# All 36 weight-sum pieces made in blocks 1 and 2 of a fused attention and gated feed-forward kernel, none in the first pair

## The chip, the cores and the metric

The kernel runs on one core of one Trainium2 chip. The metric is the device time of one execution in microseconds (us), the median of several executions; lower is better. Engines are named as the profile names them: PE (TensorE matmul) and PEld (its weight loads), DVE (VectorE), ACT (ScalarE), POOL (GpSimd) and SP (SyncE, whose queue SPq issues every DMA of this kernel).

## The reference: what is computed

Chunked attention (chunks of 64 tokens, 8 batches, 8 heads, 576 tokens, head size 64), and its output, as 4608 tokens of 512 numbers, through a gated feed-forward layer with 1536 hidden features. All in float32:

```python
scores = scale * np.matmul(q_c, k_c.transpose(0, 1, 2, 4, 3))
scores = scores - np.max(scores, axis=-1, keepdims=True)
attn = np.exp(scores)
attn = attn / (np.sum(attn, axis=-1, keepdims=True) + 1e-09)
out = np.matmul(attn, v_c)
...
x = np.ascontiguousarray(attn_out.transpose(0, 2, 1, 3)).reshape(B * S, H * D)
gate = 1.0 / (1.0 + np.exp(-(x @ w_gate)))
val = x @ w_val
return (gate * val @ w_out).astype(np.float32)
```

## The kernel before

**Tiling.** The 4608 tokens are 9 blocks of 512. Float32 products are made from a high and a low part of each operand, three matmuls for one product. Blocks 0, 1 and 2 go through the feed-forward layer directly: for each of 12 feature groups f, `up` makes the gate in PSUM buffer g0 (12 matmuls) and the value in g1 (12 matmuls), one buffer each, and `down` (12 matmuls) adds the group to four output banks `acc`. Blocks 3 to 8 go as three pairs n = 0, 1, 2, in which two blocks of tokens, two halves of features and two halves of d_model are multiplied with seven products in the place of eight (L563 and L712). For that the weights are needed in sums and differences as well, kept in DRAM.

**The pieces.** `keep_sums` (L436) makes these weight sums in 36 pieces. A piece is two or three additions on DVE (L452, or L456 and L459), five instructions on POOL (L461, L462, L463, L465, L466) and two or four DMAs on SP's queue (L470 into `sums`, L474 into `stream`). Pieces 1 to 24 are for the gate and value weights, 25 to 36 for the output weights. Two pieces share a tile `a_val`, and there are two places for it, "spare" and "p1", one buffer each, used by turns: the first DVE addition of an odd piece waits until the two pieces that had that place before are through POOL and their DMAs have landed. `a_high` takes a buffer of the tag "ob" (two buffers), which the block outputs (`evacuate`, L399) use too.

**What sets the order.** PE, DVE and ACT issue in the order in which the program is written, in blocks 1 and 2 (`rest`, L909) and in the pairs (`pairs`, L934). POOL and SP are put in order by a scheduler in blocks 1 and 2, and stand as written in the pairs. In blocks 1 and 2 a step is one feature group and has two halves; after each half `tick` and `insert` hand out parts of the attention of later blocks (`flow`, L743), and then `keep` (L901) is called with the number of pieces that are wanted by then. With h the number of the half step, counted from 2 at block 1's first, the number wanted is

```python
keep(9 * (h - 2) // 10 if h < 21 else 16 if h < 24 else min(30, h - 7))
```

so that 16 pieces are made in block 1, none while its outputs leave (h from 21 to 23), and pieces 17 to 30 in block 2, up to h = 37. The last six are made in the first pair, one or none at each of its steps, with `late=True`: the high part then stands in the same tile, and the stores are put off to the next step (`put`, L485).

**What stands around it.** `hidden` (L370) is the chain of one step: gate in g0, sigmoid on ACT (L373, frees g0), value in g1, product on DVE (L376, frees g1), high part on ACT (L379), low part on DVE (L381). At the end of block 2 the first pair's operands are made from the attention output `raw`: `differ` (L525, DVE), `operands` (L541 DVE, L545 ACT) and `lower` (L553, DVE). All of these stand in DVE's and ACT's queues between the steps' own instructions.

Of the kernel before, what the change touches and what calls it, by code (L numbers as in the profile page):

```python
# [8 lines left out]
F32 = mybir.dt.float32  # L9
F32R = mybir.dt.float32r  # L10
# [5 lines left out]
P = 128  # L16
D = 64
NB = 9
TB = 512
# [46 lines left out]
PRODUCTS = (1, 6, 2, 7, 5, 4, 3)  # L66
# [3 lines left out]
def chunk_attn_moe(ctx: ExitStack, tc: tile.TileContext, q, k, v, w, out, outt):  # L70


    nc = tc.nc

    const = ctx.enter_context(tc.tile_pool(name="const", bufs=1))
    wp = ctx.enter_context(tc.tile_pool(name="wp", bufs=1))
    xp = ctx.enter_context(tc.tile_pool(name="xp", bufs=4))
    ap2 = ctx.enter_context(tc.tile_pool(name="ap2", bufs=2))
    mp = ctx.enter_context(tc.tile_pool(name="mp", bufs=2))
# [12 lines left out]
    kp = ctx.enter_context(tc.tile_pool(name="kp", bufs=1))  # L92
# [13 lines left out]
    wt, raws, whole, made, spare, arrivals = {}, {}, {}, {}, {}, []  # L106
# [314 lines left out]
    given, sums, vals = {}, {}, {}  # L421
    stream = dp.tile([P, 7, 6, 512], F32, name="stream")

    def keep_given(p, which):

        if which == 2:
            for r, f, i in ((1, 2 * p, 0), (2, 2 * p + 1, 0), (4, 2 * p + 1, 1)):
                nc.sync.dma_start(
                    stream[:, PRODUCTS.index(r), p].rearrange("p (a n) -> p a n", a=2),
                    wt[f, 2][:, :, i * 256:(i + 1) * 256].bitcast(F32))  # L430
            return
        t = given[p, which] = dp.tile([P, 3, 2, 256], F32, name=f"given{p}{which}")
        for n, (f, k) in enumerate(((2 * p, 0), (2 * p, 1), (2 * p + 1, 1))):
            nc.sync.dma_start(t[:, n], wt[f, which][:, :, k * 256:(k + 1) * 256].bitcast(F32))

    def keep_sums(p, which, c, late=False):  # L436

        if c == 0 and which < 2:
            sums[p, which] = dp.tile([P, 2, 2, 2, 256], F32, name=f"sums{p}{which}")
        if late or c == 0:  # L440
            pool, tag = ((wp, "spare"), (kp, "p1"))[(c if late else 2 * p + which if which < 2 else p) % 2]
            vals[0] = pool.tile([P, 2, 4, P], F32, tag=tag, name="a_val")
        if late:
            val, high = vals[0][:, 0], vals[0][:, 1].rearrange("p s n -> p (s n)").bitcast(F32R)
        else:
            val, high = vals[0][:, c], mp.tile([P, TB], F32R, tag="ob", name="a_high")
        for n in range(2):
            f = 2 * p + n
            if which < 2:
                parts = wt[f, which].rearrange("p a (k c n) -> p a k c n", k=2, c=2)[:, :, :, c].bitcast(F32)  # L450
                dst = val[:, 1:3] if n else val[:, 0::3]
                nc.vector.tensor_tensor(out=dst, in0=parts[:, 0], in1=parts[:, 1], op=ALU.add)  # L452
                continue
            parts = wt[f, 2].rearrange("p a (i c n) -> p a i c n", i=2, c=2)[:, :, :, c].bitcast(F32)
            if n == 0:
                nc.vector.tensor_tensor(out=val[:, 0:2], in0=parts[:, 0], in1=parts[:, 1], op=ALU.add)  # L456
            else:
                for i, at in enumerate((3, 2)):
                    nc.vector.tensor_tensor(out=val[:, at], in0=parts[:, 0, i], in1=parts[:, 1, i], op=ALU.add)  # L459
        flat = val.rearrange("p s n -> p (s n)")  # L460
        nc.gpsimd.tensor_tensor(out=val[:, 1], in0=val[:, 1], in1=val[:, 2], op=ALU.add)  # L461
        nc.gpsimd.tensor_tensor(out=val[:, 0], in0=val[:, 1], in1=val[:, 0], op=ALU.subtract)  # L462
        nc.gpsimd.tensor_tensor(  # L463
            out=val[:, 2:4], in0=val[:, 2:4], in1=val[:, 0:1].broadcast_to([P, 2, P]), op=ALU.subtract)
        nc.gpsimd.tensor_copy(high, flat)  # L465
        nc.gpsimd.tensor_tensor(out=flat, in0=flat, in1=high.bitcast(F32), op=ALU.subtract)  # L466
        def store():
            for a, t in enumerate((high.bitcast(F32), flat)):
                if which < 2:
                    nc.sync.dma_start(sums[p, which][:, :, c, a], t.rearrange("p (h n) -> p h n", h=2))  # L470
                    continue
                for i, r in enumerate((6, 7)):
                    at = PRODUCTS.index(r)
                    nc.sync.dma_start(  # L474
                        stream[:, at:at + 4:3, p, c * 256 + a * P:c * 256 + (a + 1) * P],
                        t[:, i * 256:(i + 1) * 256].rearrange("p (s n) -> p s n", s=2))

        if late:
            stores.append(store)
        else:  # L480
            store()

    stores = []

    def put():  # L485
        while stores:
            stores.pop(0)()

    places = ["u8", "u9", "u10", "u11", "u7"]

# [384 lines left out]
    def insert(upto=4 * NB, pieces=0):  # L875


        if now["item"] in ("S", "then") or (
                now["item"] in ("A", "AS") and now["unit"] < upto and now["ticks"] >= now["since"] + pieces):
            if now["item"] in ("A", "AS"):  # L880
                release()
            advance()
# [9 lines left out]
    def step(m, f, span):  # L892
        pending.append(hidden(m, f, spans[span]))

    def finish():
        down(*pending.pop(0))
# [1 line left out]
    kept = [(p, which, c) for p in range(6) for which in range(2) for c in range(2)]  # L898
    kept += [(p, 2, c) for p in range(6) for c in range(2)]

    def keep(wanted, late=False):  # L901
        while len(kept) > 36 - wanted:
            p, which, c = kept.pop(0)
            if c == 0 and which < 2:
                with tc.issue_after(arrivals[-1].ins):
                    keep_given(p, which)
            keep_sums(p, which, c, late)

    def rest():  # L909
        with tc.issue_after(arrivals[-1].ins):  # L910
            for p in range(6):
                keep_given(p, 2)
        for m in range(1, FIRST_PAIR):
            upto = 4 * (m + 2) if m == 1 else 4 * (m + 3)
            for f in range(2 if m == 1 else 0, NF):
                if m == 2 and f == 7:
                    now["early"] = now["open"] = now["late"] = 0
                step(m, f, "")
                x = 2 * (12 * m + f - 13)
                for part in range(2):  # L920
                    if part:
                        finish()
                    tick(SHARES[m])
                    insert(upto, 1)
                    h = x + part
                    keep(9 * (h - 2) // 10 if h < 21 else 16 if h < 24 else min(30, h - 7))
                if m == 2:
                    if f == 8:
                        for which in range(2):
                            load_group(0, 0, which)  # L930
        with tc.manual_schedule(engines={mybir.EngineType.Pool, mybir.EngineType.SP}):
            pairs(keep)

    def pairs(keep):  # L934
        for n in range(3):
            now["joined"], now["late"], now["up"] = True, n, n
            upto = 4 * (FIRST_PAIR + 2 * n + 4)
            order = [(p, which) for p in range(6) for which in range(2)]
            due(n, 5)
            for i, (p, which) in enumerate(order):  # L940
                if i + 1 < len(order) and i > 0:
                    load_group(n, *order[i + 1])
                put()
                if pending:
                    banks[n, "z"] = sole(n, p, which)
                    while pending:
                        finish()
                first(n, p, which)
                if i == 0:
                    due(n, 7)  # L950
                if i == 11:
                    now["early"] = n + 1
                if i:
                    tick(SHARES["first"], "first")
                    last(n, *order[i - 1])
                    if i == 10:
                        ending = outward(n, lambda: (last(n, *order[-1]), gate()))
                        next(ending)
                    late = 30 + (0, 1, 2, 3, 3, 4, 5, 6)[min(i, 7)]
                    if n == 0 and i % 2:  # L960
                        keep(late, True)
                    tick(SHARES["last"] if i < 11 else 1.2, "last")
                    gate()
                    if n == 0:
                        keep(late, True)
                middle(n, p, which, lambda: i and insert(upto, 1))
                if i == 10:
                    next(ending)
                if i == 11:
                    now["open"] = n + 1  # L970
                if 0 < i < 11:
                    tick(SHARES["middle"], "middle")
            next(ending, None)
# [39 lines left out]
```

## Time and profile before

| | |
|---|---|
| time, median of 3 runs | 885.11 us (883.43 to 886.03) |
| the profiled execution's own time | 887.66 us |
| its span | 885.8 us |
| PE busy | 875.8 us (99%) |
| DVE, ACT, POOL busy | 625.4, 401.4, 267.1 us |
| block 1, about | 146 to 250 us from the span's start |
| block 2, about | 250 to 346 us |
| the first pair, about | 346 to 529 us |
| pieces 1 to 30 on POOL | 162.6 to 326.2 us |
| pieces 31 to 36 on POOL | 360.8 to 431.3 us |

The profile is one execution; 1.9 us of its time lie outside the span. A PE that is busy is not PE at its peak, since matmuls are pipelined, so a lost microsecond shows in three places: as idle time ahead of a PE instruction, as a group of matmuls that takes longer than the same group elsewhere, and as a granted clock below 1.00. In rows of the timeline and of the groups, the bracket or last column tells how long the engine sat idle ahead of the instruction and what ended that.

### The profile page before, as it was taken

What the parts mean: (1) busy time and instruction counts of PE and PEld (TensorE: products, weight loads), DVE (VectorE), ACT (ScalarE), POOL (GpSimd) and SP (SyncE); (2) the same over time, 40 slices, a digit from 0 to 9 for tenths busy, and PEclk for the clock granted to TensorE, in tenths of its full rate; (3) what the DMA queues carried; (4) which work ended last, traced back from release to release, by engine and by line L of the source; (5) the groups of instructions that cost most, each with busy time, mean ns of one, the idle gap of its engine ahead of it and who ended that gap; (6) DMA issues with size and microseconds to landing.
All of it is one profiled execution on the core that took longest, in us unless ns stands there. A gap on an engine that the chain in (4) does not pass through costs nothing.

```text
span 885.8 us, 15559 instructions
## 1 busy us (share of the span) xinstructions
PE 875.8 (99%) x6050; PEld 718.7 (81%) x6050; DVE 625.4 (71%) x908; ACT 401.4 (45%) x706; POOL 267.1 (30%) x329
## 2 busy tenths in 40 slices
PE   8999999999999999999999999999999999999998
PEld 4888888888888888878888888888888888888886
DVE  6999963588668865757768957666589654335874
ACT  6897662345535443345554523555245221123341
POOL 0000000497948960676720002253400002432000
PEclk9999999999999999999999999999999999999999
DMA  8675389946355477677865567666345685654453
GB/s 316 233 249 202 116 282 343 303 135 196 128 167 167 132 206 270 204 274 231 291 226 191 214 217 257 238 240 237 134 178 216 210 307 173 209 202 139 182 216 140
DMA packets 84506, 189.77 MB, mean 214 GB/s; under 512 B 7248, under 2 KB 45648, under 8 KB 80592
## 3 DMA queue, kind: packets, MB, share of 16 engines
q1 hardware_dynamic: 84432, 188.77, 61.7%
q8 instruction: 48, 0.79, 0.4%
q14 instruction: 26, 0.21, 0.1%
HBM read 146.28 MB, written 42.47 MB: 213 GB/s over the span
## 4 chain that ended last, share of the span: by engine, by line
PE 93%; DMA 3%; DVE 2%; issue 0%; ACT 0%; SPq 0%; DVEq 0%
PE g L357 22%; PE d L712 19%; PE cy L563 16%; PE cz L563 11%; PE acc L392 11%; PE cx L563 10%; PE av L212 2%; DMA w_raw<-w_in 2%; PE sc L197 2%; DMA wr<-sums 1%; DMA wr<-given 1%; DVE xc L553 0%; PE tp L281 0%; DVE raw L525 0%; DVE pr L823 0%
## 5 line engine op out<-in xcount | busy, mean ns | idle before, releaser
L357 PE MATMUL g<-xt,w 128*128 128x512 f32 (+1 forms) x960 | 206.2, 370 | 0.8 <-DVE xt L301 0.6
L357 PEld LDWEIGHTS g<-xt,w 128*128 128x128 f32 x960 | 167.5, 188 | 32.3 <-DVE xt L301 0.9
L712 PE MATMUL d<-hd,wd 128*128 128x512 f32 x756 | 172.5, 389 | 0.1
L712 PEld LDWEIGHTS d<-hd,wd 128*128 128x128 f32 x756 | 141.8, 188 | 30.3 <-DVE hd L692 0.9
L563 PE MATMUL cy<-xc,wr 128*128 128x512 f32 x648 | 159.2, 389 | 0.2 <-DMA wr<-sums 0.2
L563 PEld LDWEIGHTS cy<-xc,wr 128*128 128x128 f32 x648 | 121.6, 188 | 25.8 <-DMA wr<-sums 0.6
L563 PE MATMUL cz<-xc,wr 128*128 128x512 f32 x432 | 111.1, 393 | 0.3 <-DVE u L620 0.2
L563 PE MATMUL cx<-xc,wr 128*128 128x512 f32 x432 | 111.2, 393 | 0.0
L392 PE MATMUL acc<-w,hx 128*128 128x512 f32 x432 | 105.3, 392 | 0.0
L563 PEld LDWEIGHTS cz<-xc,wr 128*128 128x128 f32 x432 | 81.8, 190 | 18.3 <-DVE u L620 0.6
L563 PEld LDWEIGHTS cx<-xc,wr 128*128 128x128 f32 x432 | 80.8, 188 | 17.1
L392 PEld LDWEIGHTS acc<-w,hx 128*128 128x128 f32 x432 | 80.1, 188 | 16.8
L461 POOL TENSOR_TENSOR a_val<-a_val 128x128 f32<-128x128 f32 x36 | 19.7, 547 | 214.1 <-DVE a_val L452 162.8
L838 POOL COPY pt<-pr 32x256 f32<-32x256 f32 x86 | 35.9, 418 | 156.8 <-DVE pr L827 153.1
L691 ACT CAST hd<-hid 128x1024 fp32r<-128x1024 f32 x48 | 49.9, 1051 | 49.2 <-PE d L712 33.2
L579 ACT COPY s1u<-cx 128x512 f32<-128x512 f32 x36 | 21.1, 586 | 106.3 <-PE cx L563 101.9
L692 DVE TENSOR_TENSOR hd<-hid,hd 128x1024 fp32r<-128x1024 f32 x48 | 58.4, 1221 | 12.4 <-ACT hd L691 12.2
L591 POOL TENSOR_TENSOR hid<-u,hid 128x512 f32<-128x512 f32 x15 | 19.5, 1301 | 142.4 <-DVE u L620 141.7
L581 DVE TENSOR_TENSOR s1u<-cy,s1u 128x512 f32<-128x512 f32 x36 | 24.7, 685 | 39.1 <-PE cy L563 39.1
L838 ACT COPY pt<-pr 32x256 f32<-32x256 f32 x110 | 44.3, 403 | 13.1 <-DVE pr L827 11.6
L641 ACT ACTIVATE hid<-hid 128x512 f32<-128x512 f32 x54 | 32.4, 628 | 34.9 <-DVE hid L635 28.9
L620 DVE TENSOR_TENSOR hid<-cz,u 128x512 f32<-128x512 f32 x18 | 12.4, 691 | 49.6 <-PE cz L563 49.5
(118 smaller groups left out, 1144.8 us busy)
## 6 DMA issues: line engine op xcount, KB each, us to landing
wr<-sums SPq DMA_DIRECT2D x72, 512.0 KB, 5.3
wd<-stream SPq DMA_DIRECT2D x30, 1024.0 KB, 4.6
w_raw<-w_in SPq DMA_DIRECT2D x36, 512.0 KB, 4.6
wr<-given SPq DMA_DIRECT2D x36, 512.0 KB, 4.3
qt<-q_in SPq DMA_DIRECT2D x18, 512.0 KB, 4.9
kt<-k_in SPq DMA_DIRECT2D x18, 512.0 KB, 5.8
vt<-v_in SPq DMA_DIRECT2D x18, 512.0 KB, 4.1
given<-w SPq DMA_DIRECT2D x36, 256.0 KB, 4.3
```

The source lines that it names most:

```text
L357: nc.tensor.matmul(ps[:, tok], lhsT=wt[f, which][:, wpart, c:c + P], rhs=x[:, part, i, tok], start=n == 0, stop=n == 11)
L392: nc.tensor.matmul(acc[m, t], lhsT=hx[:, ts], rhs=wt[f, 2][:, wpart], start=f == 0 and i == 0, stop=f == NF - 1 and i == 2,)
L461: nc.gpsimd.tensor_tensor(out=val[:, 1], in0=val[:, 1], in1=val[:, 2], op=ALU.add)
L563: nc.tensor.matmul(bank, lhsT=lhs(wpart, c), rhs=x[:, part, c], start=start and k == 0, stop=stop and k == 5, skip_group_check=True)
L579: nc.scalar.copy(s1, x)
L581: nc.vector.tensor_tensor(out=u2, in0=y, in1=s1, op=ALU.add)
L591: eng.tensor_tensor(out=h, in0=value, in1=h, op=ALU.mult)
L641: nc.scalar.activation(h, h, AF.Sigmoid)
L691: nc.scalar.copy(t[:, 0], at)
L692: nc.vector.tensor_tensor(out=t[:, 1], in0=at, in1=t[:, 0].bitcast(F32), op=ALU.subtract)
L712: nc.tensor.matmul(bank, lhsT=w[:, o:o + P], rhs=x[:, part], start=p == 0 and opening and i == 0, stop=p == 5 and i == 2, skip_group_check ...
L838: copy = (lambda eng, dst=pb[dst, :, c, i, :], src=ps[src, h::2, k, :]: eng(dst, src))
```

## The change

`keep` is called in blocks 1 and 2 with other numbers: h pieces after half step h up to 20, 20 while block 1's outputs leave, and from h = 24 on h - 3, until 36 are made at h = 39. The first half step makes two pieces, each further one makes one. The part that made pieces in the first pair is removed, with the late form of `keep_sums` and the stores that were put off. Nothing else of the program is changed; line numbers behind the edit are lower by up to 20 (L452 is L449, L456 is L453, L525 is L511).

```diff
-    def keep_sums(p, which, c, late=False):
+    def keep_sums(p, which, c):
...
-        if late or c == 0:
-            pool, tag = ((wp, "spare"), (kp, "p1"))[(c if late else 2 * p + which if which < 2 else p) % 2]
+        if c == 0:
+            pool, tag = ((wp, "spare"), (kp, "p1"))[(2 * p + which if which < 2 else p) % 2]
             vals[0] = pool.tile([P, 2, 4, P], F32, tag=tag, name="a_val")
-        if late:
-            val, high = vals[0][:, 0], vals[0][:, 1].rearrange("p s n -> p (s n)").bitcast(F32R)
-        else:
-            val, high = vals[0][:, c], mp.tile([P, TB], F32R, tag="ob", name="a_high")
+        val, high = vals[0][:, c], mp.tile([P, TB], F32R, tag="ob", name="a_high")
...
-        def store():
-            for a, t in enumerate((high.bitcast(F32), flat)):
...
-        if late:
-            stores.append(store)
-        else:
-            store()
+        for a, t in enumerate((high.bitcast(F32), flat)):
+            if which < 2:
+                nc.sync.dma_start(sums[p, which][:, :, c, a], t.rearrange("p (h n) -> p h n", h=2))
+                continue
...
-                    keep(9 * (h - 2) // 10 if h < 21 else 16 if h < 24 else min(30, h - 7))
+                    keep(h if h < 20 else 20 if h < 24 else min(36, h - 3))
...
-            pairs(keep)
+            pairs()
...
-                put()
...
-                    late = 30 + (0, 1, 2, 3, 3, 4, 5, 6)[min(i, 7)]
-                    if n == 0 and i % 2:
-                        keep(late, True)
                     tick(SHARES["last"] if i < 11 else 1.2, "last")
                     gate()
-                    if n == 0:
-                        keep(late, True)
```

How this moves the instructions is shown at three places.

DVE near the end of block 2, before: `hf` and `hx` are the products and low parts of the steps, `raw` and `xc` the first pair's operands. The first row is the product of feature group 8.

```order
L376 TENSOR_TENSOR hf<-g_3683,hf 128x512
L381 TENSOR_TENSOR hx<-hf,hx 128x512
L525 TENSOR_TENSOR raw<-raw 128x2x512
L376 TENSOR_TENSOR hf<-g_3740,hf 128x512
L381 TENSOR_TENSOR hx<-hf,hx 128x512
L525 TENSOR_TENSOR raw<-raw 128x2x512
L553 TENSOR_TENSOR xc<-raw,xc 128x1024 x3
L541 TENSOR_TENSOR raw<-raw 128x2x512
```

The same stretch of DVE in the changed kernel:

```order
L376 TENSOR_TENSOR hf<-g_3737,hf 128x512
L381 TENSOR_TENSOR hx<-hf,hx 128x512
L453 TENSOR_TENSOR a_val<-w 128x256
L456 TENSOR_TENSOR a_val<-w 128x128 x2
L511 TENSOR_TENSOR raw<-raw 128x2x512
L453 TENSOR_TENSOR a_val<-w 128x256
L456 TENSOR_TENSOR a_val<-w 128x128 x2
L376 TENSOR_TENSOR hf<-g_3821,hf 128x512
L381 TENSOR_TENSOR hx<-hf,hx 128x512
L511 TENSOR_TENSOR raw<-raw 128x2x512
L539 TENSOR_TENSOR xc<-raw,xc 128x1024 x3
L527 TENSOR_TENSOR raw<-raw 128x2x512
```

Two pieces, 35 and 36, now stand between the low part of group 8 and the product of group 9; ahead of the first row the two orders have the same kinds of rows back to the start of block 2, with pieces numbered four higher.

SP's queue at the end of block 2, before: the stores of pieces 29 and 30, a load of v, and the loads `wr` of the first pair's first weights.

```order
L474 DMA stream<-a_high 128x2x128 x2
L474 DMA stream<-a_val 128x2x128 x2
L178 DMA vt<-v_in 128x1024
L474 DMA stream<-a_high 128x2x128 x2
L474 DMA stream<-a_val 128x2x128 x2
L501 DMA wr<-given_1865 128x1024
L504 DMA wr<-sums_1869 128x1024
L501 DMA wr<-given_1865 128x512
L504 DMA wr<-sums_1869 128x1024
```

The same place in the changed kernel, from the stores of piece 33 on:

```order
L470 DMA stream<-a_high 128x2x128 x2
L470 DMA stream<-a_val 128x2x128 x2
L178 DMA vt<-v_in 128x1024
L470 DMA stream<-a_high 128x2x128 x2
L470 DMA stream<-a_val 128x2x128 x2
L487 DMA wr<-given_1820 128x1024
L490 DMA wr<-sums_1824 128x1024
L470 DMA stream<-a_high 128x2x128 x2
L470 DMA stream<-a_val 128x2x128 x2
L470 DMA stream<-a_high 128x2x128 x2
L470 DMA stream<-a_val 128x2x128 x2
L487 DMA wr<-given_1820 128x512
```

The stores of pieces 35 and 36 now stand between the first two `wr` loads and all later ones.

SP's queue in the first pair, before, at the step whose attention loads (`vt`, `qt`, `kt`) come second in the pair:

```order
L501 DMA wr<-given_2459 128x512
L504 DMA wr<-sums_2463 128x1024
L474 DMA stream<-a_val 128x2x128 x4
L178 DMA vt<-v_in 128x1024
L170 DMA qt<-q_in 128x1024
L172 DMA kt<-k_in 128x1024
```

The same step in the changed kernel:

```order
L487 DMA wr<-given_2265 128x512
L490 DMA wr<-sums_2269 128x1024
L178 DMA vt<-v_in 128x1024
L170 DMA qt<-q_in 128x1024
L172 DMA kt<-k_in 128x1024
```

The four stores of a late piece are gone from this step, as at five others. PE's and ACT's orders are the same row for row in both kernels.

## Rows read from the trace of the kernel before

**Rows 1.** The page's first part: busy time, share of the span, instructions

```profile
PE 875.8 (99%) x6050; PEld 718.7 (81%) x6050; DVE 625.4 (71%) x908; ACT 401.4 (45%) x706; POOL 267.1 (30%) x329
```

**Rows 2.** Chain that ended last, end of block 2: start us, us, what

```profile
325.11 2.23 DVE raw L525
327.34 3.48 DVE xc L553 x3
330.82 1.15 DVE raw L541
...
332.95 0.60 ACT hf L373
...
333.59 5.73 PE g L357 x24
```

**Rows 3.** Timeline of DVE, blocks 1 and 2: start us, us, what [idle before]

```profile
159.76 0.69 DVE L376 TENSOR_TENSOR hf<-g,hf 128x512 f32<-128x512 f32 x1 [3.40 <-PE g L357]
...
254.84 0.65 DVE L376 TENSOR_TENSOR hf<-g,hf 128x512 f32<-128x512 f32 x1
...
312.39 1.02 DVE L456 TENSOR_TENSOR a_val<-w 128x256 f32<-128x256 f32 x1 [2.45 <-DMA stream<-a_val]
...
314.00 0.68 DVE L456 TENSOR_TENSOR a_val<-w 128x256 f32<-128x256 f32 x1
...
315.55 0.68 DVE L376 TENSOR_TENSOR hf<-g,hf 128x512 f32<-128x512 f32 x1
...
317.95 1.47 DVE L525 TENSOR_TENSOR raw<-raw 128x1024 f32<-128x1024 f32 x1
322.66 0.69 DVE L376 TENSOR_TENSOR hf<-g,hf 128x512 f32<-128x512 f32 x1 [3.24 <-PE g L357]
```

**Rows 4.** Timeline of POOL, blocks 1 and 2

```profile
198.42 1.81 POOL L838 COPY pt<-pr 32x256 f32<-32x256 f32 x4
...
221.14 1.85 POOL L838 COPY pt<-pr 32x256 f32<-32x256 f32 x4 [3.08 <-DVE pr L827]
...
242.76 1.29 POOL L466 TENSOR_TENSOR a_val<-a_val,a_high 128x512 f32<-128x512 f32 x1
...
316.18 1.30 POOL L466 TENSOR_TENSOR a_val<-a_val,a_high 128x512 f32<-128x512 f32 x1
...
324.64 1.61 POOL L466 TENSOR_TENSOR a_val<-a_val,a_high 128x512 f32<-128x512 f32 x1
```

**Rows 5.** Timeline of SP's queue; then landings of L474's stores, 315 to 320 us

```profile
317.50 0.89 SPq L474 DMA_DIRECT2D stream<-a_val  x2
...
DMA to landing us min/median/max: 1.9/2.3/2.6
```

**Rows 6.** DVE groups by shape: L381, L525 at 162-326, L541 at 322-342, L684 anywhere

```profile
L381 DVE TENSOR_TENSOR hx<-hf,hx 128x512 fp32r<-128x512 f32 x18 | 17.6, 977 | 13.7 <-ACT hx L379 13.7
...
L525 DVE TENSOR_TENSOR raw<-raw 128x1024 f32<-128x1024 f32 x2 | 3.8, 1890 | 0.0
...
L541 DVE TENSOR_TENSOR raw<-raw 128x1024 f32<-128x1024 f32 x3 | 3.7, 1218 | 0.0
...
L684 DVE TENSOR_TENSOR hd<-hid,hd 128x512 fp32r<-128x512 f32 x30 | 19.6, 684 | 0.7 <-ACT hd L683 0.5
```

**Rows 7.** Timeline of PE in the first pair; its chain; windows with PEclk

```profile
385.30 1.65 PE L563 MATMUL cz<-xc,wr 128*128 128x512 f32 x6 [0.17 <-DVE u L620]
...
393.23 0.39 PE L197 MATMUL sc<-kt,qt 64*64 64x64 f32 x10 [1.65 <-issue]
...
393.62 2.07 PE cx L563 x6
395.69 2.48 PE cz L563 x6
398.17 1.36 PE cx L563 x6
...
395.00:396.00 1.00, 1.00 (x4) 0.74 (x3) 0.00 (x0) 0.27 (x1) 0.92 (x2) 0.50 0.67 262
```

**Rows 8.** Chain that ended last, where block 1's outputs leave

```profile
253.21 5.44 PE g L357 x24
```

More of the change, by code (lines that the diff above doesn't have):

```diff
@@ L466, in keep_sums @@
         nc.gpsimd.tensor_tensor(out=flat, in0=flat, in1=high.bitcast(F32), op=ALU.subtract)
-        def store():
-            for a, t in enumerate((high.bitcast(F32), flat)):
[L469 to L476, printed above, removed]
-        if late:
-            stores.append(store)
-        else:
-            store()
[L483 to L487, printed above, removed]
+        for a, t in enumerate((high.bitcast(F32), flat)):
+            if which < 2:
+                nc.sync.dma_start(sums[p, which][:, :, c, a], t.rearrange("p (h n) -> p h n", h=2))
+                continue
+            for i, r in enumerate((6, 7)):
+                at = PRODUCTS.index(r)
+                nc.sync.dma_start(
+                    stream[:, at:at + 4:3, p, c * 256 + a * P:c * 256 + (a + 1) * P],
+                    t[:, i * 256:(i + 1) * 256].rearrange("p (s n) -> p s n", s=2))
     places = ["u8", "u9", "u10", "u11", "u7"]
@@ L899, in chunk_attn_moe, with keep @@
     kept += [(p, 2, c) for p in range(6) for c in range(2)]
-    def keep(wanted, late=False):
+    def keep(wanted):
         while len(kept) > 36 - wanted:
@@ L906, in keep @@
                     keep_given(p, which)
-            keep_sums(p, which, c, late)
+            keep_sums(p, which, c)
     def rest():
@@ L931, in rest, with pairs @@
         with tc.manual_schedule(engines={mybir.EngineType.Pool, mybir.EngineType.SP}):
-            pairs(keep)
-    def pairs(keep):
+            pairs()
+    def pairs():
         for n in range(3):
```

## The prediction, made before the changed kernel was run

> **What bounds the kernel now.** First the page's busy times: PE is busy for 875.8 of 885.8 us [rows 1]. No microsecond of DVE, ACT or POOL counts unless PE comes to wait for it, so the question is not how much work is moved (none is removed) but where PE's cover is thin. Second the chain of work that ended last, which is PE nearly throughout. The place in blocks 1 and 2 where it leaves PE is 322.6 to 333.6 us, at the end of block 2 [rows 2]: DVE makes L525, three L553 and an L541 back to back, ACT then casts and does the sigmoid L373 of feature group 10, and only then may PE write g0 for group 11, at 333.59. The start of that chain is DVE's product of group 9 at 322.66, which waited 3.24 us for PE [rows 3]. So DVE has 3.24 us of slack just ahead of 322.66 and none behind it, up to 333.59. Third, PE in the first pair, where six pieces are made now: it waits 0.17 us for a DVE result at 385.30, and 1.65 us at 393.23 for nothing that the profile shows; behind that gap its granted clock is 0.50, the 1.2 GHz level, and two groups of six matmuls take 2.07 and 2.48 us where the next takes 1.36 [rows 7].
>
> **What the change removes.** Six late pieces leave the first pair: on DVE each costs about 1.6 us (piece 29 from 312.39 to 314.00, piece 30 from there to 315.55 [rows 3]), on POOL about 4.1 us: five pieces and five `pt` copies run from 221.14 to 242.76 + 1.29 = 244.05, 22.9 us [rows 4]; the copies, at 1.85 us for four, are 2.3 of it, and (22.9 - 2.3) / 5 = 4.1. That is 10 us of DVE and 25 us of POOL, beside a PE that waited for DVE there for 0.17 us [rows 7]. I credit 0.2. The 1.65 us gap and the 1.83 us behind it (2.07 + 2.48 - 2 x 1.36 [rows 7]) are named by the profile as no one's; PE's order, row for row, is unchanged, and the loads of v, q and k beside the gap stay. I take it to stay, credit 0, and keep -3.5 as the other end.
>
> **Early pieces.** Three pieces come in the first two steps of block 1, where DVE still waits 3.40 us for PE [rows 3]; their 4.8 us spread over two steps. Nothing on PE, since it does not wait for DVE there. Loads of q and k in SP's queue now stand behind stores of pieces 1 to 5, and are used a step or more later: 0.
>
> **Block 1.** Four pieces more are made by the pause. From the `pt` copies at 198.42 to those at 221.14 there are now five pieces and not four, and five took 22.9 us elsewhere [rows 4]: POOL is through at 198.42 + 22.9 = 221.3, where the copies now start at 221.14 after 3.08 us of idleness. POOL's slack is used up and it is 0.2 us late. Behind that, both orders have five pieces up to the pause, so piece 20 ends 0.2 us later than piece 16 does now. On it hangs a chain: store of the piece, the load of v behind it in SP's queue, four output stores, DVE's output copy, and then the product L376 at 254.84, ready at 255.49. PE wants it for the next value matmuls, 2.72 us into the 24 that start at 253.21 [rows 8], at 255.93. Cover 0.44 against 0.2 late: I take 0. The other end, should five pieces take 1 us more, is a wait of 0.8.
>
> **End of block 2.** From the start of block 2 to the low part of group 8, DVE's order has the same rows with pieces numbered four higher, so I read piece 28's times for 32. Then pieces 35 and 36 stand where DVE was idle, with L525 between them. Piece 35 needs the place "p1" from pieces 31 and 32. Piece 28's last POOL instruction runs from 316.18 to 317.48 [rows 4], its two last stores are issued from 317.50 to 318.39, and such stores land 1.9 to 2.6 us after issue, median 2.3 [rows 5]; the second, issued about 317.95, lands at 320.2. The same wait is seen on piece 29 now: 2.45 us, ended by such a store [rows 3]. So DVE stands idle from 317.95 to about 320.3, and then does piece 35 (1.6), L525 (1.47) and piece 36 (1.6): 325.0. The product of group 9 starts at 325.0 and not at 322.66: **2.3 us late**. Behind the waiting addition in DVE's queue stand exactly the instructions of the chain that ends at PE. Without the wait for the place the three would end at 317.95 + 4.7 = 322.65, just in time; it is the wait, not the work, that costs.
>
> To this comes POOL. Now it is done with piece 30 at 326.25 [rows 4]; with two more pieces it works to 326.25 + 2 x 4.1 = 334.5, all through the chain, which runs beside an idle POOL now. DVE instructions with two inputs in SBUF are slower beside a busy POOL: L381 takes 977 ns there and its twin L684 684 (+0.29), L525 1890 where L541 of the same shape takes 1218 (+0.67) [rows 6]. Three L553 and one L541 are newly exposed. Ends: 4 x 0.29 = 1.2 and 4 x 0.67 = 2.7; L525 is the nearest by shape but is two instances, L381 is eighteen, so I take the middle, **1.9**. Together g0 comes free 2.3 + 1.9 = 4.2 us later, and PE, which already waits at 333.59, has no cover. ACT's and DVE's other work shifts alike and adds nothing.
>
> The Trainium skill's page "SBUF — State Buffer", section "Who interferes with whom", gives the mechanism: a DVE instruction with two SBUF inputs contends with a GpSimd instruction that reads SBUF, and whoever holds the shared port keeps it for its whole instruction. The trace agrees that such instructions are longer and not by how much: by that rule each of the four could be held for a whole L466 of 1.3 us, 5.2 in all, and the time by it would be 3.3 us above mine.
>
> After a gap of 1.65 us PE's clock fell and cost 1.83 us [rows 7]. After one of 4.2 us I expect the same, **1.8**; the other end is 0, since matmuls of full size and not small ones precede this gap.
>
> The later `wr` loads stand behind the stores of pieces 35 and 36, at about 335 us; the first of them to be used, beyond the two ahead of those stores, is wanted about 350 by PE's order. No cost.
>
> **Sum.** 4.2 + 1.8 - 0.2 = +5.8 us. On the profiled execution: 887.66 + 5.8 = 893.5. That execution lies 2.55 us above the median of the runs; on the median, 885.11 + 5.8 = **890.9 us**. With the low ends (2.3 + 1.2 - 0.2) it is 888.4, with the high ones (2.3 + 2.7 + 1.8 - 0.2) 891.7.
>
> **The rivals.**
> - *The delay does not reach PE.* If the stores of piece 32 land by 318 us or the two pieces are shorter than piece 29, the product of group 9 is on time; DVE then has only POOL's company to pay, and that too may be half. For it: the work itself fits 3.24 us of slack but for the wait. Against it: 1.9 us is the fastest landing seen in that stretch. Time: 885.11 - 0.2 = 884.9, no change.
> - *Faster, on the other side: the gap of the first pair goes.* If PE's 1.65 us are a late delivery of its instructions by DMA, they may go with the late pieces' stores, which are issued shortly ahead; the clock then doesn't fall, and the pair gives 1.65 + 1.83 + 0.2 = 3.7 us. It decides the sign if the delay at 322 us is under 3.7. For it: this is the one such gap of the kernel and lies among the late pieces. Against it: PE's order, and the loads right beside the gap, stay. With the first rival: 881.4. With my delay: 885.11 + 6.0 - 3.7 = 887.4.
> - *Block 1's outputs.* If POOL's five pieces take 1 us more, PE waits 0.8 us at 255.9 besides: 891.7.
>
> **How the numbers follow.** From 885.11, a measurement of this kernel can tell 0.3%, 2.7 us. The delay reaches PE and the gap stays: 0.54, 888.4 to 891.7, slower. The delay reaches PE and the gap goes: 0.10, 887.4, within 0.3%. No delay, gap stays: 0.22, 884.9, within. No delay and no gap: 0.14, 881.4, faster. So slower 0.54, same 0.32, faster 0.14. The range leaves out the last case and covers the others with the unknown costs: 883.5 to 893.5; the likeliest case alone is 888 to 892.5.
>
> **What would show it.** In the trace after: DVE idle ahead of the first addition of piece 35, ended by a store of `stream`; the product of group 9 later than PE's end of its value matmuls by 2 us or so; POOL busy until about 334; an idle PE of 3 to 5 us ahead of the gate matmuls of group 11, ended by the sigmoid, and a granted clock of 0.50 behind it. Wrong if PE shows no wait between 320 and 340 us; wrong in its credit if the 1.65 us gap in the first pair is gone.

## The result and the profile after

The changed kernel takes 896.64 us (median; 894.97 to 897.57), the kernel before, run beside it, 885.87 us (883.43 to 886.53): a ratio of 1.0125, interval 1.0105 to 1.0144, or 9 to 13 us more. The prediction was 890.9 us, with a range up to 893.5. It had the sign and the place at the end of block 2; it missed a second loss, in block 1, whose two steps it had put at nothing.

PE has no more work than before [rows 1] and is now busy for a smaller share. The page of the changed kernel, busy time and the chain that ended last by engine:

```profile
PE 876.9 (98%) x6050; PEld 718.8 (80%) x6050; DVE 632.9 (71%) x908; ACT 401.6 (45%) x706; POOL 272.4 (30%) x329
...
PE 68%; DVE 11%; POOL 8%; issue 5%; DMA 4%; ACT 3%; SPq 1%; POOLq 0%; ACTq 0%; DVEq 0%
```

In the kernel before, PE is 93% of that chain; at 68% the chain leaves PE for long stretches, so PE waited there. Where it waited is read from the timeline of PE (start, length, line, in brackets the idle time ahead of the row and what ended it). These are all its rows from 100 us to the end that have a bracket:

```profile
202.88 3.02 PE L357 MATMUL g<-xt,w 128*128 128x512 f32 x12 [1.27 <-DVE hf L376]
209.63 1.17 PE L212 MATMUL av<-pt,vt 64*64 64x64 f32 x62 [0.76 <-POOL a_val L459]
237.09 5.73 PE L357 MATMUL g<-xt,w 128*128 128x512 f32 x24 [0.26 <-ACT hf L373]
256.25 1.65 PE L392 MATMUL acc<-w,hx 128*128 128x512 f32 x6 [1.26 <-DVE ob L410]
261.05 3.02 PE L357 MATMUL g<-xt,w 128*128 128x512 f32 x12 [0.41 <-DVE hf L376]
291.85 1.17 PE L212 MATMUL av<-pt,vt 64*64 64x64 f32 x62 [0.31 <-POOL a_val L460]
344.49 7.13 PE L357 MATMUL g<-xt,w 128*128 128x512 f32 x24 [5.05 <-ACT hf L373]
```

The kernel before has one such row up to the first pair, 0.16 us ahead of the gate matmuls at 333.59 (the last of [rows 2]); those 24 matmuls took 5.73 us behind it and take 7.13 here. So there are two losses: **block 1 and its end**, 4.27 us in six short waits (1.27 + 0.76 + 0.26 + 1.26 + 0.41 + 0.31, the last of them in block 2), and **the end of block 2**, 5.05 us and 1.40 of slower matmuls. The idle times are not the whole loss, since a group behind a wait runs a little longer too. As PE's order is the same in both kernels, the start of the same group can be compared: one in the middle of block 2 and the one behind the slow matmuls, before and then after:

```profile
299.31 5.60 PE L357 MATMUL g<-xt,w 128*128 128x512 f32 x24
...
339.16 2.88 PE L392 MATMUL acc<-w,hx 128*128 128x512 f32 x12
```

```profile
305.32 5.60 PE L357 MATMUL g<-xt,w 128*128 128x512 f32 x24
...
351.46 2.88 PE L392 MATMUL acc<-w,hx 128*128 128x512 f32 x12
```

The changed kernel is 6.0 us late at the first place and 12.3 at the second: 6.0 us are lost in block 1 and behind it, 6.3 at the end of block 2. At the end of the span it is only 8.1 us late (893.9 for 885.8), mostly because the gap of [rows 7] in the first pair is absent here. The medians differ by 10.8. One other execution of the kernel before has that gap with 1.33 us (see the last experiment); how much of it the rest had is not on record, so the 12.3 and the 10.8 can't be brought closer together.

The end of block 2 reads as the prediction has it. DVE of the changed kernel, from the low part of group 8 on (compare [rows 2, 3]):

```profile
323.04 0.79 DVE L381 TENSOR_TENSOR hx<-hf,hx 128x512 fp32r<-128x512 f32 x1 [0.69 <-ACT hx L379]
325.76 0.46 DVE L453 TENSOR_TENSOR a_val<-w 128x256 f32<-128x256 f32 x1 [1.92 <-DMA stream<-a_val]
...
327.91 1.75 DVE L511 TENSOR_TENSOR raw<-raw 128x1024 f32<-128x1024 f32 x1
329.58 0.83 DVE L453 TENSOR_TENSOR a_val<-w 128x256 f32<-128x256 f32 x1
...
332.11 0.68 DVE L376 TENSOR_TENSOR hf<-g,hf 128x512 f32<-128x512 f32 x1
...
336.77 4.55 DVE L539 TENSOR_TENSOR xc<-raw,xc 128x1024 fp32r<-128x1024 f32 x3
```

DVE sits idle for 1.92 us ahead of piece 35's first addition, which is let go by a store; the product of group 9 has no bracket, so it is late for PE and not PE for it; the three L539 take 4.55 where L553 took 3.56 in the timeline of before.

Block 1's loss starts at 184 us, on DVE. First DVE, then SP's queue, then the DMA traffic and the `a_val` stores from 180 to 190 us (size, median from issue to landing), all of the changed kernel:

```profile
190.23 0.76 DVE L449 TENSOR_TENSOR a_val<-w 128x256 f32<-128x256 f32 x2 [6.23 <-issue]
190.91 0.68 DVE L376 TENSOR_TENSOR hf<-g,hf 128x512 f32<-128x512 f32 x1
```

```profile
175.71 4.71 SPq L434 DMA_DIRECT2D given<-w  x7
180.53 0.65 SPq L170 DMA_DIRECT2D qt<-q_in  x1
181.22 0.68 SPq L172 DMA_DIRECT2D kt<-k_in  x1
182.00 0.52 SPq L466 DMA_DIRECT2D sums<-a_high  x1
182.63 0.55 SPq L466 DMA_DIRECT2D sums<-a_val  x1
```

```profile
DMA packets 2491, 3.19 MB, mean 319 GB/s; under 512 B 167, under 2 KB 2233, under 8 KB 2489
...
sums<-a_val SPq DMA_DIRECT2D x2, 256.0 KB, 6.5
```

The row at 190.23 is the first addition of piece 9, whose place was piece 6's; piece 6's last store is the one issued at 182.63, behind seven `given` stores and two loads. Of the two stores in that median it is the slower one: it lands 7.5 us after its issue, at 190.1, and the addition starts 0.1 us later. (The bracket's "issue" only says that the wait was not put down to it.) In the kernel before the same kind of store in the same ten microseconds lands in 2.4 us, among 107 GB/s:

```profile
DMA packets 1089, 1.07 MB, mean 107 GB/s; under 512 B 64, under 2 KB 1088, under 8 KB 1088
...
sums<-a_val SPq DMA_DIRECT2D x2, 256.0 KB, 2.4
```

The `given` stores are L434's, 36 of 256 KB: the plain weights that the pairs need beside the sums. `keep` hands them out with each second piece of these weights, so a change of its numbers moves them too. The kernel before issues 33 of them ahead of the first store of a piece; in the changed kernel 13 stand among the stores of pieces 3 to 8. SP's queue and the product L376 in the kernel before:

```profile
155.16 7.17 SPq L434 DMA_DIRECT2D given<-w  x10
165.58 0.60 SPq L470 DMA_DIRECT2D sums<-a_high  x1
...
170.54 1.68 SPq L434 DMA_DIRECT2D given<-w  x3
```

```profile
186.23 0.68 DVE L376 TENSOR_TENSOR hf<-g,hf 128x512 f32<-128x512 f32 x1
```

The same product, behind the waiting addition, starts 4.7 us later in the changed kernel (190.91), and from there DVE and POOL run late up to PE's wait at 202.88.

### The profile page after: what moved, and what is told of

Read it like the earlier page. It is cut to its first block, busy times and chain, and to the rows that moved or that the text cites. A ratio compares the mean times of both kernels' runs of the same rounds, so it can differ in the third digit from the quotient of the medians.

```text
span 893.9 us, 15561 instructions
## 1 busy us (share of the span) xinstructions
PE 876.9 (98%) x6050; PEld 718.8 (80%) x6050; DVE 632.9 (71%) x908; ACT 401.6 (45%) x706; POOL 272.4 (30%) x329
## 4 chain that ended last, share of the span: by engine, by line
PE 68%; DVE 11%; POOL 8%; issue 5%; DMA 4%; ACT 3%; SPq 1%; POOLq 0%; ACTq 0%; DVEq 0%
PE cy L549 16%; PE d L698 12%; PE cx L549 11%; PE cz L549 11%; PE g L357 9%; PE acc L392 4%; POOL a_val L463 2%; DMA w_raw<-w_in 2%; POOL a_high L462 2%; POOL a_val L460 1%; PE av L212 1%; DMA sums<-a_val 1%; POOL a_val L458 1%; DVE hid L687 1%; DVE xc L539 1%
## 5 line engine op out<-in xcount | busy, mean ns | idle before, releaser
L357 PE MATMUL g<-xt,w 128*128 128x512 f32 (+1 forms) x960 | 208.4, 372 | 7.6 <-ACT hf L373 5.3
L458 POOL TENSOR_TENSOR a_val<-a_val 128x128 f32<-128x128 f32 x36 | 21.9, 608 | 158.8 <-DMA given<-w 153.1
L678 DVE TENSOR_TENSOR hd<-hid,hd 128x1024 fp32r<-128x1024 f32 x48 | 58.4, 1222 | 12.4 <-ACT hd L677 12.2
L463 POOL TENSOR_TENSOR a_val<-a_val,a_high 128x512 f32<-128x512 f32 x36 | 50.3, 1397 | 2.1
```

The costliest lines, as they stand in the source:

```text
L357: nc.tensor.matmul(ps[:, tok], lhsT=wt[f, which][:, wpart, c:c + P], rhs=x[:, part, i, tok], start=n == 0, stop=n == 11)
L678: nc.vector.tensor_tensor(out=t[:, 1], in0=at, in1=t[:, 0].bitcast(F32), op=ALU.subtract)
```

## Experiments

Each was measured beside runs of the kernel before, as a ratio; a difference in us below is what the ratio has over 1, times 885. Its interval is 1 to 2 us to either side, as the brackets show. The changed kernel is at +11.1 on that scale.

**The end of block 2.** Three kernels take it apart. First without its last two pieces in blocks 1 and 2, in the form of the kernel before:

```diff
-keep(9 * (h - 2) // 10 if h < 21 else 16 if h < 24 else min(30, h - 7))
+keep(h if h < 20 else 20 if h < 24 else min(34, h - 3))
-late = 30 + (0, 1, 2, 3, 3, 4, 5, 6)[min(i, 7)]
+late = 34 + (0, 1, 2)[min(i, 2)]
```

> Changed kernel, but the last two pieces, 35 and 36, are made in the first pair as the kernel before makes its last six. Theory: in the trace of the changed kernel PE waits 5.05 us ahead of the gate matmuls of group 11 (344.49 us) and those matmuls take 7.13 us where they take 5.44 in the kernel before, because these two pieces stand ahead of the product of group 9; without them both go: 896.6 - 5.05 - 1.69 = 889.9 us. Rival: the wait is POOL's or the earlier delays' doing (block 1 is unchanged here, pieces 33 and 34 still stand at the end of block 2): 895 to 897.

Measured: 889.18 us, ratio 1.0047 (1.0031 to 1.0063), +4.2. The wait is gone; the gate matmuls of group 11 have no bracket and stand at 5.68:

```profile
339.67 5.68 PE L357 MATMUL g<-xt,w 128*128 128x512 f32 x24
```

So the two pieces cost 11.1 - 4.2 = 6.9 us, and two late pieces in the first pair show no wait of PE but the 0.36 us of the gap treated below. Next, both pieces stay, with a place of their own:

```diff
+            if (p, which) == (5, 2):
+                pool, tag = wp, "o0"
             vals[0] = pool.tile([P, 2, 4, P], F32, tag=tag, name="a_val")
```

> Changed kernel, but pieces 35 and 36 get a place of their own for a_val, the tile of the output weights of feature group 0, which nothing needs there any more. Theory of the prediction: the wait for the place (1.92 us of idle DVE ahead of piece 35) is passed on whole: PE's wait of 5.05 us falls to about 3.1, the time to 894.7; what stays is POOL's company and the clock. Rival 1: without the wait the two pieces fit the slack, all 6.7 us go: 889.9. Rival 2: the wait hides behind POOL, nothing goes: 896.6.

Measured: 892.95 us, 1.0089 (1.0071 to 1.0107), +7.9: 3.2 less, between the first two cases. And then the same without these pieces' work on POOL:

```diff
+        whole_piece = (p, which) != (5, 2)
+        if not whole_piece:
+            high = flat.bitcast(F32R)
-        nc.gpsimd.tensor_tensor(...)
+        whole_piece and nc.gpsimd.tensor_tensor(...)
```

(and so for all five instructions).

> The variant in which pieces 35 and 36 have a place of their own, and without the five POOL instructions of each of these two pieces: both stores take DVE's unsplit sums, so the weights of these two pieces are wrong. It measures POOL's company by itself. Theory: the DVE rows between the product of group 9 and the gate matmuls of group 11 return to what they take in the kernel before (L525 2.31, three L553 3.56, L541 1.22 us; with the variant's L541 at 4.72 and L529 at 2.31 us that is 2.2 us less), so PE's wait falls from 2.77 to about 0.6 us and the time from 893.0 to about 890.5 us. Rival: POOL's company costs nothing of it and the two pieces' DVE time does: 893.0 us.

Measured: 889.33 us, 1.0047 (1.0030 to 1.0065), +4.2: 3.7 less again. (The weights of these two pieces are wrong in it; it serves for the time alone.) PE of the variant with its own place, and of that one without POOL's work:

```profile
342.12 7.07 PE L357 MATMUL g<-xt,w 128*128 128x512 f32 x24 [2.77 <-ACT hf L373]
```

```profile
339.12 5.74 PE L357 MATMUL g<-xt,w 128*128 128x512 f32 x24 [0.32 <-ACT hf L373]
```

And their DVE rows on the chain, in the same order:

```profile
332.14 1.48 DVE L513 TENSOR_TENSOR raw<-raw 128x1024 f32<-128x1024 f32 x1
333.54 4.72 DVE L541 TENSOR_TENSOR xc<-raw,xc 128x1024 fp32r<-128x1024 f32 x3
338.18 2.31 DVE L529 TENSOR_TENSOR raw<-raw 128x1024 f32<-128x1024 f32 x1
```

```profile
331.66 1.21 DVE L516 TENSOR_TENSOR raw<-raw 128x1024 f32<-128x1024 f32 x1
332.79 3.57 DVE L544 TENSOR_TENSOR xc<-raw,xc 128x1024 fp32r<-128x1024 f32 x3
336.27 1.22 DVE L532 TENSOR_TENSOR raw<-raw 128x1024 f32<-128x1024 f32 x1
```

The wait of 5.05 us is thus 2.28 for the place (5.05 to 2.77), 2.45 for POOL's company (2.77 to 0.32; the three DVE rows differ by 2.51), and 0.32 that is left. The slow matmuls behind it stay while the wait is 2.77 us (7.07) and go with POOL's company (5.74): 2.45 of waiting and 1.33 of slow matmuls are 3.8 us, and the time falls by 3.7.

**Block 1.** The changed kernel does two things there at once: pieces begin two steps earlier, and 20 and not 16 are made by the pause. First both, in the kernel before, with nothing else changed:

```diff
-keep(9 * (h - 2) // 10 if h < 21 else 16 if h < 24 else min(30, h - 7))
+keep(h if h < 20 else 20 if h < 28 else min(30, h - 7))
```

> Kernel before, but with the changed kernel's rate in block 1 alone: 20 pieces by the pause, then none until the old count is reached, 30 pieces by the end of block 2, six in the first pair as before. Theory: the waits seen in block 1 of the changed kernel (1.27 + 0.76 + 0.26 + 1.26 + 0.41 = 4.0 us) come with this rate alone: 885.9 + 4.0 = 889.9 us. Rival (the prediction's step): block 1's cover just holds, 885.9 to 886.7.

Measured: 889.32 us, 1.0050 (1.0034 to 1.0066), +4.4. It shows the changed kernel's waits one by one (1.29, 0.71, 0.52, 1.15, 0.44 us at 203, 210, 238, 257, 261). With the 6.9 us of the two last pieces that is 11.3 for the 11.1 measured: within the intervals the two losses are the whole result. Then the early start alone, `keep(h if h < 16 else 16 if h < 24 else min(30, h - 7))`:

> Kernel before, but one piece for each half step from block 1's first on until 16 are made, as in the changed kernel; then none until the old count asks for the 17th; 30 pieces by the end of block 2, six in the first pair. It parts the early start from the four pieces more. Theory: pieces that start while SP's queue is full of given stores wait for their own stores (place of piece 9), so the two waits of PE at 203 and 210 us (1.28 and 0.72 us, each with about 0.3 us of slower matmuls behind it) stay, and those at 237 to 261 us go: 884.4 + 2.6 = 887.0 us. Rival: the number of pieces by the pause makes all the waits: 884.4 us.

Measured: 887.48 us, 1.0028 (1.0017 to 1.0039), +2.5. Its waits of PE in blocks 1 and 2:

```profile
202.81 3.03 PE L357 MATMUL g<-xt,w 128*128 128x512 f32 x12 [1.19 <-DVE hf L376]
209.56 1.17 PE L212 MATMUL av<-pt,vt 64*64 64x64 f32 x62 [0.74 <-POOL a_val L462]
237.41 5.76 PE L357 MATMUL g<-xt,w 128*128 128x512 f32 x24 [0.65 <-ACT hf L373]
```

So the waits at 203, 210 and 237 us are the early start's, those at 256 and 261 the number's. The one at 237 was expected to go and stays. By the times, the early start is 2.5 us of the 4.4 and the number the other 1.9. The number without the early start, but with the old slow start and 11 pieces in the last eight half steps, `keep(9 * (h - 2) // 10 if h < 12 else h - 3 + (h - 12) // 3 if h < 20 else 20 if h < 28 else min(30, h - 7))`:

> Kernel before with its own slow start (9 pieces by half step 12) and then 20 pieces by the pause, the 21st when the old count asks for it; 30 by the end of block 2, six in the first pair. The four pieces more without the early start. Theory: no wait at 203 us; POOL, with 11 pieces of about 4.1 us in 8 half steps of about 4.7 us, is late at the pause, and the chain piece 20, its store, output stores, output copy makes PE wait 1.3 us or more at 256 us: 884.4 + 2 = 886.4 us or more. Rival (only the early start hurts): 884.4 us.

Measured: 898.51 us, 1.0153 (1.0134 to 1.0171), +13.5: far worse than the changed kernel's even rate, with six waits from 229 to 264 us, the last three of 1.82, 2.24 and 2.45 us around the output copies. An even rate is the better way to make 20; how much of the 13.5 is the number and how much the crowding, this run doesn't tell.

Then SP's queue. All `given` stores ahead of the pieces:

```diff
             for p in range(6):
-                keep_given(p, 2)
+                for which in range(3):
+                    keep_given(p, which)
```

> Changed kernel, but all stores of given weights (L434) are handed to SP's queue at the start of block 1, ahead of the stores of the pieces, where the kernel before has nearly all of them too. Theory: block 1's waits of PE (1.27 + 0.76 + 0.26 + 1.26 + 0.41 us) come from piece 9's addition, which waits 6.2 us for the stores of piece 6 that stand in SP's queue behind given stores; with the queue cleared they shrink to 1 us or less: 896.6 - 3 = 893.6 us. Rival: it is the four pieces more in block 1 and POOL's work for them, not the queue: the waits and 896.6 stay.

Measured: 899.85 us, 1.0168 (1.0151 to 1.0186), +14.9: a miss, and a telling one. No `given` store stands between the pieces' stores now, but the first of them stand behind the whole bulk. An addition on DVE waits 9.28 us, up to 173.01, and PE has new waits earlier, of 1.42 and then 1.61 us:

```profile
175.88 3.03 PE L357 MATMUL g<-xt,w 128*128 128x512 f32 x12 [1.42 <-DVE hf L376]
```

So the interleaving is not needed for the loss: it is enough that pieces begin while the DMA engines still have the bulk to move. The other way round, each two pieces' `given` stores behind the pieces' own (`marks[-1]` is the last store of a piece):

```diff
-                with tc.issue_after(arrivals[-1].ins):
-                    keep_given(p, which)
             keep_sums(p, which, c)
+            if c == 1 and which < 2:
+                with tc.issue_after(marks[-1].ins):
+                    keep_given(p, which)
...
-            for p in range(6):
-                keep_given(p, 2)
...
+                    if f < 6:
+                        with tc.issue_after(marks[-1].ins):
+                            keep_given(f, 2)
```

> Changed kernel, but the given stores of a pair of pieces are issued on SP's queue behind the two pieces' own stores, and those of the output weights in block 2, so that no store of a piece stands behind a bulk of given stores. Theory: piece 9's wait of 6.2 us on DVE and with it PE's waits at 203 and 210 us go (1.27 + 0.76 and 0.3 us of slower matmuls behind each), those at 237 to 261 us shrink, the end of block 2 stays: 896.6 - 2.6 = 894.0, down to 890.6 if all of block 1's waits go. Rival: it is POOL's load in block 1 that counts (85.8 us busy of 110 where the kernel before has 68.1): 896.6 us.

Measured: 895.01 us, 1.0115 (1.0095 to 1.0136), +10.2. Piece 9's wait falls from 6.23 to 1.13 us, the waits at 203, 210, 237 and 261 us are gone and the one at the end of block 2 is down to 1.83 + 0.62; there is a new one of 0.80 at 316, and the one at 256 has become 6.07:

```profile
257.94 2.93 PE L392 MATMUL acc<-w,hx 128*128 128x512 f32 x6 [6.07 <-DVE ob L410]
```

It is this kernel's own doing: three `given` and two `stream` stores now stand at the pause, ahead of the load of v and the output stores, and DVE's second output copy waits 9.87 us for an output store where it waited 7.19 in the kernel before. So the last two kernels keep the pause clear: the stores of the output weights at the start of block 1, `given` behind the pieces for `p < 3`, the rest one tile a step in block 2. On the variant with a place of its own for pieces 35 and 36:

> The variant in which pieces 35 and 36 have a place of their own (892.95 us), with the given stores handed out: those of the output weights at the start of block 1, then one tile of three stores behind each second piece for the first twelve pieces, and one tile for each step of block 2 from its second on; none at the pause. All 36 pieces are still made in blocks 1 and 2. Theory: all of block 1's waits go (six waits of 4.3 us in sum and about 0.3 us of slower matmuls behind each): 893.0 - 6 = 887 us, with the wait of 2.8 us at the end of block 2 left. Rival: 20 pieces by the pause are too much for POOL however the stores stand: the waits at 256 and 261 us (1.6 and 0.4 us) stay: 889.5 us.

Measured: 891.45 us, 1.0086 (1.0069 to 1.0103), +7.6: above both expectations. Its waits of PE up to the end of block 2, and POOL's last row ahead of the pause:

```profile
253.05 1.66 PE L392 MATMUL acc<-w,hx 128*128 128x512 f32 x6 [1.32 <-DVE ob L410]
257.85 3.02 PE L357 MATMUL g<-xt,w 128*128 128x512 f32 x12 [0.42 <-DVE hf L376]
310.75 1.17 PE L212 MATMUL av<-pt,vt 64*64 64x64 f32 x62 [0.41 <-DVE pr L784]
339.70 3.01 PE L357 MATMUL g<-xt,w 128*128 128x512 f32 x12 [3.06 <-ACT hf L373]
343.19 3.02 PE L357 MATMUL g<-xt,w 128*128 128x512 f32 x12 [0.47 <-DVE hf L376]
```

```profile
245.03 1.29 POOL L465 TENSOR_TENSOR a_val<-a_val,a_high 128x512 f32<-128x512 f32 x1
```

With the queue clear the waits at 203, 210 and 237 us are gone: they were the early start's, through the queue. Those behind the pause stay, 1.32 + 0.42, as the rival had it. PE is on the time of the kernel before up to there, so POOL can be compared directly: piece 20 ends at 246.32, where piece 16 ended at 242.76 + 1.29 = 244.05 [rows 4], 2.27 us later, and the product L376 behind the pause starts at 257.14 where it started at 254.84 [rows 3], 2.30 later. The time itself, +7.6 for +7.9, is not lower by more than the intervals leave open. The `given` stores in block 2 come with new waits (0.41 at 310.75, and 3.06 + 0.47 for 2.77 at the end). With pieces 35 and 36 late:

> The variant in which pieces 35 and 36 are made in the first pair (889.2 us), with the given stores handed out in the same way. Theory: the two causes, stores of pieces behind given stores in block 1 and pieces 35 and 36 ahead of the product of group 9, are all there is: 884.4 us, the kernel before, within 1 us. Rival: what POOL has to do by the pause costs by itself: 886.5 us or more.

Measured: 888.21 us, 1.0045 (1.0030 to 1.0060), +4.0: the rival's case. Of it 1.35 + 0.41 us are waits of PE behind the pause and 0.38 + 0.81 new ones at 305 and 312 us, in block 2. No variant beats the kernel before.

That block 1's early waits come through SP's queue is thus shown by the traces: they are gone in all three kernels that clear it. That clearing it gains time is not shown: 11.1 became 10.2, 7.9 became 7.6 and 4.2 became 4.0, each within the intervals, with new waits in the place of the old ones.

**The gap in the first pair.** The kernel before once more:

> The kernel before, unchanged, profiled once more. Theory: PE's gap of 1.65 us in the first pair and the slow matmuls behind it belong to that one profiled execution (the variants with late pieces show 0.36 and 0.25 us there, with a time 2.5 us over the median for the execution with the gap): the gap is 0.4 us or less and the span about 882.5 us. Rival: it belongs to the late pieces: 1.65 us again, 885.8 us.

Measured: 884.82 us, span 883.0; the gap is there with 1.33 us and without slow matmuls behind it:

```profile
391.71 0.39 PE L197 MATMUL sc<-kt,qt 64*64 64x64 f32 x10 [1.33 <-issue]
```

Neither expectation holds. At that place the variant with both changes in block 1 has 0.25 us, the one with two late pieces 0.36, the one with paced stores (no late piece) 0.35, and the two others with six late pieces have no such row, nor has the changed kernel. So late pieces are neither needed for it nor enough, and its size differs between executions of one program; what makes it is open. It cost 1.65 + 1.83 us in the profiled execution of before [rows 7], which lies 2.55 us above the median of its runs.

## Why the prediction was half right

The end of block 2 came as predicted. The sum failed at the step on early pieces, which put their cost at 0, and at the term for block 1's pause, which it put at 0 too.

- **End of block 2.** Right, in mechanism and size. It said 2.3 us for the place, 1.9 for POOL's company, 1.8 for the clock, 6.0 in all. The runs gave 2.28, 2.45, and 1.40 (7.13 less 5.73), 6.1 in the trace; the time without the two pieces is 6.9 lower. The company lay near the upper end of 1.2 to 2.7. POOL was to work until 334.5 and worked until 344.0: the piece ahead of the two ends 5.3 us later than was read for it (331.57 for 326.25), as PE itself is 6.0 us late there from block 1, and the two pieces took 12.4 us for the 8.2 in the sum, beside a busy DVE. The granted clock behind the gap was 0.79 on average and not 0.50, and the loss 1.40 and not 1.8. The Trainium skill's rule ("SBUF — State Buffer", "Who interferes with whom") gave an estimate of 5.2 us for the four rows by whole POOL instructions; the two variants differ by 2.24 there (4.72 and 2.31 for 3.57 and 1.22).
- **Early pieces: the step that failed first.** It said that three more pieces in the first steps cost nothing since DVE waits for PE there [rows 3], and that loads of q and k behind their stores are used later. Both hold. But the step followed only what stands behind the new stores in SP's queue, and not what the new stores themselves stand behind, nor who waits for them: the next two pieces at that place, whose first addition stands ahead of the step's product in DVE's queue. That is the very wait that the prediction priced for piece 35. Piece 9's addition waited 6.23 us for a store that took 7.5 us behind the bulk, and the early start alone cost 2.5 us (1.5 to 3.5). The row to look at was in reach: the `given` stores of before, issued to about 172 us, with pieces made slowly up to then. The Trainium skill's page "DMA: Bandwidth & Descriptors", section "Queues, rings and completion order", says that descriptors are consumed in ring order on each DMA engine; the trace agrees as far as it goes: the two loads issued at 180.53 and 181.22 land at 185.8 and 187.5, and piece 6's last store, issued at 182.63 behind them, at 190.1.
- **Block 1's pause: mechanism right, term mis-sized.** The chain from piece 20 over the stores of the outputs to the product was named, with a cover of 0.44 us. POOL's lateness was put at 0.2 us, from five pieces in 22.9 us; with the queue clear it is 2.27. Of that 0.44 was covered, and PE waits 1.32 + 0.42 = 1.74; the first of the two waits is for the output copy itself, ahead of the product. By the times the four pieces more cost 1.9 us (4.4 less 2.5). In the variant with the clear queue five pieces and the copies take 24.4 us, from 198.66 to 223.10, and not 22.9. That DVE, which is busy for 25.6 of the 30 us from 190 to 220 there, slows POOL throughout is not borne out: the first four pieces take 18.9 us with their copies (198.66 to 217.60), and so they do in the kernel before (198.42 to 218.06, less 0.70 of waiting), beside a DVE that is busy for 26.2 of the same 30 us. The excess lies in the fifth, which takes 5.2 us where the prediction's mean was 4.1, with a last instruction of 2.15 us where the other four have 1.27 to 1.29, and in 0.35 us behind it in which POOL waits for DVE. What makes that instruction long is not tested. The other end, 0.8, was under half of the wait.
- **First pair.** Taken as staying, the gap is gone from the profile of after, by 3.5 us of that execution. By the prediction's own sign its credit is then wrong, but it can't be booked as a gain of the change either: two variants with six late pieces don't have the gap. The credit of 0.2 is not borne out: the three variants of block 1 that keep six late pieces don't have the wait of 0.17 us either.
- **The sum.** By the times, 6.9 us for the two last pieces and 4.4 for block 1 are 11.3, where 11.1 was measured on that scale; the prediction had 5.8 and 0. The range was too narrow because of the two steps that were costed at zero: the early pieces had no upper end at all, and that of the pause was less than half of what it cost.

## What to carry to other kernels

A step that issues stores is not free because the engines have slack: find what its stores queue behind, how long they then take to land, and which instruction waits in order for the buffer that they free. When work is packed more densely, a mean duration from another stretch needs an upper end: here one piece of 5.2 us, where the mean was 4.1, was more than a slack of 0.44 bears. Give every zero in the sum such an end. For 20 pieces an even rate with an early start (+4.4) was better than a late crowd (+13.5); for 16 the slow start of the kernel before was 2.5 us better than the early one.

## What the hardware showed beyond that

- DVE and POOL slow each other in both directions. DVE's rows get shorter when POOL's work is taken away (4.72 to 3.57 us for the three of `lower`). The other direction is read from rows alone: beside DVE's L527 and the next L539, POOL's last instruction of piece 36 takes 2.12 us where [rows 4] has 1.29 to 1.61:

```profile
341.86 2.12 POOL L463 TENSOR_TENSOR a_val<-a_val,a_high 128x512 f32<-128x512 f32 x1
```

- PE's clock behind a gap doesn't follow the length of the gap. Behind 5.05 us of waiting the granted clock is 0.79 on average from 344 to 352 us, so at the 1.2 GHz level for part of it and at 2.4 GHz for the rest, and 24 matmuls cost 1.4 us more; behind 2.77 us in the variant with its own place 0.82 and 1.3 us; behind 3.06 us in the one with the queue cleared it stays at 1.00; behind 1.65 us it fell to 0.50 [rows 7], the 1.2 GHz level, and behind 1.33 us at the same place it did not. Nor is it the same in every execution of one program: of four of the variant with the queue cleared, two have a mean clock of 1.000 over the span (890.34 and 890.83 us) and two 0.998 (892.07 and 892.48); of the changed kernel's five, two have 0.998 (894.97 and 895.65) and three 0.996 (896.64 to 897.57). The windows of the changed kernel and of that with the queue cleared (stretch, busy time of PE, PEld, DVE, ACT and POOL, PEclk, DMA share, GB/s):

```profile
344.00:352.00 8.00, 7.51 (x27) 6.13 (x28) 7.31 (x8) 3.52 (x5) 0.00 (x0) 0.79 0.80 240
```

```profile
339.50:347.50 8.00, 7.33 (x31) 5.76 (x32) 7.31 (x7) 3.13 (x5) 4.65 (x4) 1.00 0.33 88
```
